# Two fused feed-forward blocks behind linear attention: where the tiles lie in SBUF

## The chip, the cores and the metric

The kernel runs on one core of a Trainium2 chip. The metric is the device time of one execution in microseconds, as the median of several runs; beside it stands one execution recorded by the hardware profiler, and all durations of single instructions come from that one.

## The reference

For 8 batches, 8 heads, 576 positions and 64 features per head:

```
kv  = einsum(k, v)                 # per head, 64 x 64
out = q @ kv                       # linear attention, no softmax
x   = out / rms(out) * g_norm      # then 4608 tokens x 512
h   = x @ w_in                     # 512 -> 2048
g   = P(h) / (Q(h) + 1e-6)         # cubic over 1 + |b0||h| + |b1|h^2
y   = g @ w_out                    # 2048 -> 512
z   = silu(y @ w_gate) * (y @ w_val)   # 512 -> 1536, two products
o   = z @ w_o2                     # 1536 -> 512
```

All data is float32.

## The kernel before

Every large product is made exact to float32 by splitting both factors into a high and a low part and multiplying three times (`mm3`, L103 to L107: high by high, high by low, low by high). All tiles are 128 partitions deep; the 4608 tokens are 9 tiles of 512. A matmul names two things in SBUF: the weights that are loaded into the array and the operand that is streamed past them (the moving operand).

**Stage 1** (to about 916 us) is a loop over 144 steps, 9 tiles of tokens by 16 chunks of `w_in`/`w_out`. A step runs 12 matmuls of `h_mm` (tile `ph`; weights `wt` in pool `w`, moving operand `x` in pool `x`) and 12 of `y_mm` for the chunk two steps earlier (tile `y`; weights `wt`, moving operand `ghl` in pool `g`). Between them, in small pieces, stands the attention of the next tile (tiles `qhl`, `kvh`, `kvl`, `sqhl` in pool `attn`). ScalarE, VectorE and GpSimd work out the rational function and write `ghl`. `y` goes to DRAM.

**Stage 2** (916 to about 1457 us) makes the gate and value products in 12 chunks of `w_gate`/`w_val`. A chunk's weights are a unit `u0` to `u5` (tile `wu`, 14 KiB per partition: seven 256-wide blocks as high and low part; chunks 6 to 11 use the units again). Token tiles, split, lie in a rotation of nine slots of 8 KiB (`slots`, L498: four in pool `x`, five in pool `ring`), and `x_slot` hands them out in turn. Three token tiles go "direct" (`direct_mm`, L584: for each of 6 chunks f and 3 tiles n, 24 matmuls, with x slots 0 to 5 as moving operand); the others go in pairs through a Strassen-like scheme of seven products of 6 matmuls (`product`, L601; 48 steps, 6 of them with 256 columns in place of 512). The first direct products stand between the last two `y_mm` of stage 1 (L880 to L884).

**Stage 3** (from 1457 us) multiplies by `w_o2`: the roles change, weights are the token slots, and the moving operand `wo` lies in the units `u0` to `u5`, three chunks in each (`o_mm`, L721).

What the vector engines do between the products is a hand-written order: `put(q, f, n, op)` hangs an operation behind step n of chunk f. In the direct part, chunk f+1's raw weights (pool `late`, tags `crg` and `crv`, two buffers each) are fetched by `u_fetch` (L437, on SyncE's queue), prepared by `u_scale` and `u_join`, split into the unit by `u_direct` (L464: two ScalarE copies and two GpSimd subtractions of 512 columns), and summed by `u_early` (four VectorE operations of 256 columns) into `sm` tiles, which `u_late` later splits into the rest of the unit. `u_direct(0)` runs in the last tile of stage 1.

Pools are stacks from two sides: a pool with `side="left"` lies above the ones opened before it, one with `side="right"` below them. By the pools' sizes a partition is laid out so (KiB from its start):

| | stage 1 | stages 2 and 3 |
|---|---|---|
| left, rising | const 1 to 2.8, w 2.8 to 130.8, g to 138.8, e to 150.8, stg to 158.8 | const, out 2.8 to 10.8, work to 24.8, ring to 64.8, raw to 88.8, units u1 to u5 to 158.8 |
| right, falling | x 192 to 224, attn 164 to 192 | x 192 to 224, late 162 to 192 (crg, crv, and u0 at 178 to 192) |

In pool `attn`, `kvh` and `kvl` lie at 164 to 172 and `qhl` and `sqhl` at 178 to 182.

Of the kernel before, what the change touches and what calls it, by code (L numbers as in the profile page):

```python
# [8 lines left out]
F32 = mybir.dt.float32  # L9
F32R = mybir.dt.float32r  # L10
# [30 lines left out]
def fused_kernel(ctx: ExitStack, tc: tile.TileContext, kv_main, kv_left, q_t, w_in, w_out, w_gate, w_val, w_o2, ab, g_norm, out):  # L41
# [14 lines left out]
    PS = bass.MemoryType.PSUM  # L56

    const = ctx.enter_context(tc.tile_pool(name="const", bufs=1, side="left"))
    a_ctx = ExitStack()
    w_p = a_ctx.enter_context(tc.tile_pool(name="w", bufs=1, side="left"))  # L60
    g_p = a_ctx.enter_context(tc.tile_pool(name="g", bufs=2, side="left"))
    e_p = a_ctx.enter_context(tc.tile_pool(name="e", bufs=2, side="left"))
    s_p = a_ctx.enter_context(tc.tile_pool(name="stg", bufs=2, side="left"))
    x_p = ctx.enter_context(tc.tile_pool(name="x", bufs=1, side="right"))
    d_p = ctx.enter_context(tc.tile_pool(name="dram", bufs=1, space=bass.MemoryType.DRAM))
    ps_y = ctx.enter_context(tc.tile_pool(name="ps_y", bufs=1, space=PS))
    ps_h = ctx.enter_context(tc.tile_pool(name="ps_h", bufs=2, space=PS))
# [35 lines left out]
    def mm3(ps, wh, wl, xh, xl, first, last, more=False):  # L103

        nc.tensor.matmul(ps, lhsT=wh, rhs=xh, start=first, stop=False, skip_group_check=more)  # L105
        nc.tensor.matmul(ps, lhsT=wh, rhs=xl, start=False, stop=False, skip_group_check=more)  # L106
        nc.tensor.matmul(ps, lhsT=wl, rhs=xh, start=False, stop=last, skip_group_check=more)  # L107
# [254 lines left out]
            c = slice(m * P, m * P + P)  # L362
            mm3(yps[m], w[:, 0, c], w[:, 1, c], g[:, 0, :], g[:, 1, :], f == 0, f == NF1 - 1)

    def evac_pair(dst, j, pool, tag, alone=False):
        sb = pool.tile([P, 2, N], F32, tag=tag, name="sb")
        act(sb[:, 0, :], yps[2 * j])
        if alone:
            nc.sync.dma_start(out=dst[:, 0, :], in_=sb[:, 0, :])
        nc.vector.tensor_copy(out=sb[:, 1, :], in_=yps[2 * j + 1])  # L370
        if alone:
            nc.sync.dma_start(out=dst[:, 1, :], in_=sb[:, 1, :])
        else:
            nc.sync.dma_start(out=dst, in_=sb)

    def y_evac(t, pool, tag):
        for j in range(2):
            evac_pair(y_dram[t][j], j, pool, tag)

    mid = {}  # L380

# [44 lines left out]
    def halves_of(ap):  # L426
        return ap.rearrange("p (a n) -> p a n", a=2)
# [2 lines left out]
    HK = DM // 2  # L430
    raw_u = {}
    val = {}
    sums = {}
    wu = {}
    w_dram = {f: d_p.tile([P, 2, N], F32, name=f"wd{f}") for f in range(UP, NF2)}
# [12 lines left out]
    def u_join(f, compact=False):  # L448

        if not compact:  # L450
            run(join_ops(raw_u[f]), 2)
            val[f] = [w_views(r)[2] for r in raw_u.pop(f)]
            return
        c = late["out"].tile([P, 2, N], F32, tag="g", name="wc")
        for j, r in enumerate(raw_u.pop(f)):
            lo, hi, _ = w_views(r)
            stt(c[:, j, :].bitcast(I32), hi, 3, lo, ALU.logical_shift_left, ALU.bitwise_or)
        nc.sync.dma_start(out=w_dram[f], in_=c)

    def u_halves(u, src, at, eng):  # L460
        act(u[:, 0, at, :], src)
        sub(eng, u[:, 1, at, :], src, u[:, 0, at, :])

    def u_direct(f, eng):  # L464

        g, v = val[f]
        u = wu[f] = late[f"u{f % UP}"].tile([P, 2, 7, HK], F32R, tag=f"u{f % UP}", name="wu")
        u_halves(u, halves_of(g), slice(0, 7, 6), eng)
        u_halves(u, halves_of(v), slice(4, 6), eng)

    def u_sums(f, tiles):
# [110 lines left out]
        return bank["d"][m % 2 * 2:m % 2 * 2 + 2]  # L582

    def direct_mm(f, n, ps, parts=2, part=0):  # L584
        u = wu[f]
        for b, at in ((0, (0, 6)), (1, (4, 5)))[part:part + parts]:
            for j in range(2):
                for kk in range(2):
                    c, x = slice(kk * P, kk * P + P), xc["D", 2 * n + j]
                    first, last = j + kk == 0, j + kk == 2  # L590
                    mm3(ps[b], u[:, 0, at[j], c], u[:, 1, at[j], c], x[:, kk, 0, :], x[:, kk, 1, :], first, last)
        return ps

    def direct_post(f, n, ps):
# [14 lines left out]
    def wid(i):  # L609
        return width[seq[steps[i][0]]]  # L610
# [17 lines left out]
    def post(i, n):  # L628

        if i < 0:  # L630
            return
        if n == 0:
            merge(i, 2, "c", ALU.subtract, "d")
            merge(i, 3, "c")
        elif n == 2:
            sv[i, "g"] = late["out"].tile([P, 2, wid(i)], F32, tag="g", name="gout")
            act(sv[i, "g"][:, 0, :], sv[i, "d"], AF.Silu)
            act(sv[i, "g"][:, 1, :], sv[i, "c"], AF.Silu)
        elif n == 3:
            g = sv[i, "g"]  # L640
            mul(g[:, 0, :], g[:, 0, :], sv[i, "a"])
        elif n == 4:
            g, (q, f) = sv[i, "g"], steps[i]
            merge(i, 3, "b")
            mul(g[:, 1, :], g[:, 1, :], sv[i, "b"])
            for h, (t, o) in enumerate(halves[seq[q]]):
                nc.sync.dma_start(out=g_dram[t, f][:, o:o + wid(i)], in_=g[:, h, :])
# [87 lines left out]
    def o_evac(n):  # L735
        t = order[n]
        o = out[t * N:(t + 1) * N, :].rearrange("(j m p) n -> j p m n", j=2, p=P)
        for m in range(4):
            yps[m] = banks(len(steps) + n)[m]
        for j in range(2):  # L740
            evac_pair(o[j], j, late["out"], "g", n == TILES - 1)

    with tc.manual_schedule():
        nc.vector.memset(bias_r, EPS_RMS)
# [89 lines left out]
        for s in range(S1):  # L834
            t, f = divmod(s, NF1)
            if s == S1 - NF1:
                attn_ctx.close()
                late["p"] = late["u0"] = ctx.enter_context(tc.tile_pool(name="late", bufs=1, side="right", reuse_waits="tile"))
                u_fetch(0)
                u_fetch(1)  # L840
            done = kv_n[1]
            h_mm(s)
            if s >= LAG:
                y_mm(s - LAG)
            attn_pe(s)
            if t == TILES - 1 and f == 2:
                u_scale(0)
            if kv_b:
                kv_evac(*kv_b)
                kv_b = None  # L850
            if t == 0 and f in (0, 3, 4, 7, 8, 11):
                pkv = ps_a.tile([P, HP, P], F32, tag="pa1", name="pkv")
                kv_b = (kv_jobs[kv_n[1]][0], pkv)
                for _ in range(HP):
                    kv_mm(pkv)
            g_step(s, raws[:2] if t == 0 else raw_u[0][f - 3:f - 2] if t == TILES - 1 and 3 <= f < 5 else ())
            if s >= LAG and f == LAG - 1:
                y_evac((s - LAG) // NF1, s_p, "stg")
            attn_tail(s)
            if t == 0:  # L860
                k = len(raws[:2])
                wa_split(k)
                for w in raws[:2]:
                    w_scale(w)
                wa_fetch(2)
                kv_load(4, done)
            if t == TILES - 1:
                if f == 5:
                    val[0] = [w_views(r)[2] for r in raw_u.pop(0)]
                    u_direct(0, nc.gpsimd)  # L870
                elif f in (6, 7):
                    raw_x["D", f - 6] = y_fetch(0, f - 6, 0, N, s_p, "stg")
                    xc["D", f - 6] = x_slot(N)
                elif 8 <= f < 12:
                    k, c = divmod(f - 8, 2)
                    split(xc["D", k][:, c, :, :], raw_x["D", k][:, c, :], nc.gpsimd)
                elif f == 12:
                    u_scale(1)
# [7 lines left out]

        a_ctx.close()
        b_pools = {}
        for name in ("out", "work", "ring", "raw", "units"):
            b_pools[name] = ctx.enter_context(  # L890
                tc.tile_pool(name=name, bufs=2 if name == "out" else 1, side="left", reuse_waits="tile")
            )
        late.update(b_pools)
        for f in range(1, UP):
            late[f"u{f}"] = b_pools["units"]
        DVE, POOL = nc.vector, nc.gpsimd

        for n, tag in enumerate(("b11", "b12", "b21", "b22"), 2):
            raw_x["D", n] = y_fetch(n // 2, n % 2, 0, N, late["raw"], tag)
        for n in range(2, 4):  # L900
            x_split(("D", n), raw_x["D", n], DVE)
        direct_post(0, 0, direct_ps)
        for n in range(4, 6):
            x_split(("D", n), raw_x["D", n], DVE)
        u_early(0)
        y_evac(TILES - 1, late["out"], "g")


        for f in range(UP):
            nxt = f + 1 < UP  # L910
            if nxt:
                if f:
                    put(0, f, 0, partial(u_scale, f + 1), partial(u_late, f - 1, DVE))
                put(0, f, 0, partial(u_join, f + 1), partial(u_direct, f + 1, POOL))
                put(0, f, 1, partial(u_early, f + 1))
                put(0, f, 2, partial(u_scale, UP + f), partial(u_join, UP + f, True))
            put(0, f, 0, partial(u_fetch, UP + f))
            if nxt and f + 2 < UP:
                put(0, f, 1, partial(u_fetch, f + 2))
        put(0, UP - 1, 0, partial(u_late, UP - 2, DVE))  # L920
        put(1, 0, 3, partial(u_scale, NF2 - 1))
        put(1, 0, 5, partial(u_join, NF2 - 1, True))
# [174 lines left out]
```

## Time and profile before

| what | value |
|---|---|
| time, median of 3 runs | 1763.37 us (1760.73 to 1764.11) |
| time of the profiled execution | 1761.45 us |
| its span, first to last instruction | 1759.7 us |
| mean granted TensorE clock | 0.999 |
| busy share of TensorE / VectorE / ScalarE / GpSimd | 99% / 70% / 57% / 29% |

TensorE's matmuls overlap: one lasts about 390 ns in the record, and the next begins some 230 ns after it. So what a matmul costs in a stretch in which TensorE never pauses is read from the stretch's length and the number of matmuls in it, not from the mean duration. The number that the view gives for a stretch takes in the matmul that is still running when the stretch begins, so one is taken off.

### The profile page before, as it was taken

What the parts mean: (1) busy time and instruction counts of PE and PEld (TensorE: products, weight loads), DVE (VectorE), ACT (ScalarE), POOL (GpSimd) and SP (SyncE); (2) the same over time, 40 slices, a digit from 0 to 9 for tenths busy, and PEclk for the clock granted to TensorE, in tenths of its full rate; (3) what the DMA queues carried; (4) which work ended last, traced back from release to release, by engine and by line L of the source; (5) the groups of instructions that cost most, each with busy time, mean ns of one, the idle gap of its engine ahead of it and who ended that gap; (6) DMA issues with size and microseconds to landing.
All of it is one profiled execution on the core that took longest, in us unless ns stands there. A gap on an engine that the chain in (4) does not pass through costs nothing.

```text
span 1759.7 us, 21291 instructions
## 1 busy us (share of the span) xinstructions
PE 1739.4 (99%) x7792; PEld 1419.9 (81%) x7792; DVE 1235.6 (70%) x1625; ACT 998.2 (57%) x1662; POOL 505.0 (29%) x361
## 2 busy tenths in 40 slices
PE   8998999999999999999999999999999999999999
PEld 6776888888888888888888888888888888888887
DVE  5989999998989898998886656756546756212211
ACT  5777777787877787777773434444424445112110
POOL 3556444444434343443331212223102212000000
PEclk9999999999999999999999999999999999999999
DMA  9763100010101000011117436122542255423411
GB/s 307 246 211 110 36 12 32 13 37 13 37 12 37 12 31 12 13 48 37 60 37 259 178 132 269 66 96 72 182 165 102 102 186 194 177 96 123 165 48 48
DMA packets 68681, 176.50 MB, mean 100 GB/s; under 512 B 7649, under 2 KB 10209, under 8 KB 66785
## 3 DMA queue, kind: packets, MB, share of 16 engines
q1 hardware_dynamic: 68576, 175.15, 28.4%
q8 instruction: 61, 1.00, 0.2%
q14 instruction: 44, 0.35, 0.1%
HBM read 117.44 MB, written 57.67 MB: 100 GB/s over the span
## 4 chain that ended last, share of the span: by engine, by line
PE 51%; issue 1%; DVE 0%; DMA 0%; POOL 0%; ACT 0%; SPq 0%; DVEq 0%; POOLq 0%; ACTq 0%
PE pb L105 10%; PE pb L107 10%; PE pb L106 10%; PE pb L731 6%; PE pb L733 6%; PE pb L732 6%; PE y L106 1%; PE y L107 1%; PE y L105 1%; PE ph L106 1%; PE ph L107 1%; PE ph L105 1%; DVE e L424 0%; DMA yraw<-yd 0%; POOL xc L94 0%
## 5 line engine op out<-in xcount | busy, mean ns | idle before, releaser
L94 POOL TENSOR_TENSOR ghl<-e,ghl 128x512 fp32r<-128x512 f32 x144 | 190.9, 1326 | 473.7 <-issue 261.6
L105 PE MATMUL pb<-xc,wu 128*128 128x512 f32 (+1 forms) x816 | 310.9, 381 | 1.0 <-DVE e L424 1.0
L107 PE MATMUL pb<-xc,wu 128*128 128x512 f32 (+1 forms) x816 | 310.8, 381 | 0.0
L106 PE MATMUL pb<-xc,wu 128*128 128x512 f32 (+1 forms) x816 | 310.6, 381 | 0.0
L101 DVE SCALAR_TENSOR_TENSOR e<-e,e 128x512 f32<-128x512 f32 x288 | 257.3, 893 | 34.5 <-ACT e L91 29.6
L106 PE MATMUL y<-ghl,wt 128*128 128x512 f32 x576 | 226.5, 393 | 4.0 <-POOL ghl L94 3.9
L105 PE MATMUL ph<-x,wt 128*128 128x512 f32 x576 | 229.6, 399 | 0.0
L106 PE MATMUL ph<-x,wt 128*128 128x512 f32 x576 | 227.3, 395 | 1.1 <-POOL x L94 1.1
L107 PE MATMUL ph<-x,wt 128*128 128x512 f32 x576 | 227.5, 395 | 0.0
L105 PE MATMUL y<-ghl,wt 128*128 128x512 f32 x576 | 225.7, 392 | 1.6 <-ACT ghl L91 1.6
L107 PE MATMUL y<-ghl,wt 128*128 128x512 f32 x576 | 226.4, 393 | 0.0
L424 DVE TENSOR_TENSOR e<-e,pb 128x512 f32<-128x512 f32 (+1 forms) x192 | 124.5, 653 | 144.1 <-PE pb L107 87.9
L91 ACT ACTIVATE e<-pb 128x512 f32<-128x512 f32 (+1 forms) x144 | 82.2, 571 | 238.7 <-PE pb L107 225.6
L105 PEld LDWEIGHTS pb<-xc,wu 128*128 128x128 f32 x816 | 153.3, 188 | 32.5 <-DVE e L424 1.6
L106 PEld LDWEIGHTS pb<-xc,wu 128*128 128x128 f32 x816 | 153.3, 188 | 31.1
L107 PEld LDWEIGHTS pb<-xc,wu 128*128 128x128 f32 x816 | 153.2, 188 | 30.9
L732 PE MATMUL pb<-wo,xc 128*128 128x512 f32 x432 | 169.3, 392 | 0.0
L731 PE MATMUL pb<-wo,xc 128*128 128x512 f32 x432 | 169.3, 392 | 0.0
L733 PE MATMUL pb<-wo,xc 128*128 128x512 f32 x432 | 169.2, 392 | 0.0
L91 ACT ACTIVATE e<-ph 128x512 f32<-128x512 f32 x144 | 85.6, 595 | 137.5 <-PE ph L107 136.9
L370 DVE COPY sb<-pb 128x512 f32<-128x512 f32 x18 | 12.5, 692 | 201.7 <-PE pb L733 201.7
L101 DVE SCALAR_TENSOR_TENSOR e<-e,na,e 128x512 f32<-128x512 f32 x144 | 148.0, 1028 | 0.0
(120 smaller groups left out, 3130.8 us busy)
## 6 DMA issues: line engine op xcount, KB each, us to landing
graw<-gd SPq DMA_DIRECT2D x108, 256.0 KB, 4.6
gd<-gout SPq DMA_DIRECT2D x84, 256.0 KB, 2.0
kvm<-in_kv_main SPq DMA_DIRECT2D x32, 512.0 KB, 9.1
yraw<-yd SPq DMA_DIRECT2D x26, 512.0 KB, 5.5
q<-in_q_t SPq DMA_DIRECT2D x36, 256.0 KB, 2.6
yd<-sb SPq DMA_DIRECT2D x18, 512.0 KB, 3.4
wraw<-in_w_in SPq DMA_DIRECT2D x16, 512.0 KB, 6.5
wraw<-in_w_out SPq DMA_DIRECT2D x16, 512.0 KB, 4.0
```

The source lines that it names most:

```text
L91: nc.scalar.activation(out=out, in_=in_, func=func, **kw)
L94: eng.tensor_tensor(out=out, in0=a, in1=b.bitcast(F32), op=ALU.subtract)
L101: nc.vector.scalar_tensor_tensor(out=out, in0=in0, scalar=scalar, in1=in1, op0=op0, op1=op1)
L105: nc.tensor.matmul(ps, lhsT=wh, rhs=xh, start=first, stop=False, skip_group_check=more)
L106: nc.tensor.matmul(ps, lhsT=wh, rhs=xl, start=False, stop=False, skip_group_check=more)
L107: nc.tensor.matmul(ps, lhsT=wl, rhs=xh, start=False, stop=last, skip_group_check=more)
L370: nc.vector.tensor_copy(out=sb[:, 1, :], in_=yps[2 * j + 1])
L424: eng.tensor_tensor(out=out, in0=a, in1=b, op=op)
L731: nc.tensor.matmul(b[m], lhsT=gh, rhs=w[:, 0, :], start=f == 0, stop=False)
L732: nc.tensor.matmul(b[m], lhsT=gh, rhs=w[:, 1, :], start=False, stop=False)
L733: nc.tensor.matmul(b[m], lhsT=gl, rhs=w[:, 0, :], start=False, stop=f == NF2 - 1)
```

## The change

The pools are laid out anew, and little else is done. In stage 1 pool `x` moves from the top to right above `const`, and `w`, `g`, `e` and `stg` move up by its 32 KiB. In stages 2 and 3 the left side is, from below, `x`, `ring`, `units` with all six units, `raw`, `work`; pool `out` is gone, and its tag `g` (results on their way out) lies in `late`, at the top. By the pools' sizes:

| | stage 1 | stages 2 and 3 |
|---|---|---|
| left, rising | const 1 to 2.8, x 2.8 to 34.8, w to 162.8, g to 170.8, e to 182.8, stg to 190.8 | const, x 2.8 to 34.8, ring to 74.8, units u0 to u5 to 158.8, raw to 182.8, work to 196.8 |
| right, falling | attn 196 to 224 | late 200 to 224 (crg, crv, g) |

Because `u0` now lies where stage 1's `w` still is, chunk 0's direct weights are split into two tiles of tag `g` first (`u_first`), its direct products read those, and `u_again` writes the three of the blocks that later products need into `u0` once stage 1 is over; `u_early(0)` moves behind `u_early(1)`. The raw token tiles for the second and third direct tile go into two ring slots in place of `raw`, and the last `y` leaves through two tags of `raw`.

```diff
     const = ctx.enter_context(tc.tile_pool(name="const", bufs=1, side="left"))
+    x_p = ctx.enter_context(tc.tile_pool(name="x", bufs=1, side="left"))
     a_ctx = ExitStack()
...
-    x_p = ctx.enter_context(tc.tile_pool(name="x", bufs=1, side="right"))
...
-    def evac_pair(dst, j, pool, tag, alone=False):
-        sb = pool.tile([P, 2, N], F32, tag=tag, name="sb")
+    def evac_pair(dst, j, pool, tag, bufs, alone=False):
+        sb = pool.tile([P, 2, N], F32, tag=tag, bufs=bufs, name="sb")
...
-        c = late["out"].tile([P, 2, N], F32, tag="g", name="wc")
+        c = late["p"].tile([P, 2, N], F32, tag="g", bufs=2, name="wc")
...
+    def u_first(eng):
+
+        for src in val[0]:
+            t = late["p"].tile([P, 2, 2, HK], F32R, tag="g", bufs=2, name="wu0")
+            act(t[:, 0], halves_of(src))
+            sub(eng, t[:, 1], halves_of(src), t[:, 0])
+            first_u.append(t)
+
+    def u_again(eng):
+
+        g, v = val[0]
+        u = wu[0] = late["u0"].tile([P, 2, 7, HK], F32R, tag="u0", name="wu")
+        u_halves(u, halves_of(g)[:, 1:2, :], slice(6, 7), eng)
+        u_halves(u, halves_of(v), slice(4, 6), eng)
...
     def direct_mm(f, n, ps, parts=2, part=0):
-        u = wu[f]
-        for b, at in ((0, (0, 6)), (1, (4, 5)))[part:part + parts]:
+        def w(b, hl, j, c):
+            return wu[f][:, hl, ((0, 6), (4, 5))[b][j], c] if f else first_u[b][:, hl, j, c]
+
+        for b in range(part, part + parts):
...
-                    mm3(ps[b], u[:, 0, at[j], c], u[:, 1, at[j], c], x[:, kk, 0, :], x[:, kk, 1, :], first, last)
+                    mm3(ps[b], w(b, 0, j, c), w(b, 1, j, c), x[:, kk, 0, :], x[:, kk, 1, :], first, last)
...
-            sv[i, "g"] = late["out"].tile([P, 2, wid(i)], F32, tag="g", name="gout")
+            sv[i, "g"] = late["p"].tile([P, 2, wid(i)], F32, tag="g", bufs=2, name="gout")
...
-            evac_pair(o[j], j, late["out"], "g", n == TILES - 1)
+            evac_pair(o[j], j, late["p"], "g", 2, n == TILES - 1)
...
-                late["p"] = late["u0"] = ctx.enter_context(tc.tile_pool(name="late", bufs=1, side="right", reuse_waits="tile"))
+                late["p"] = ctx.enter_context(tc.tile_pool(name="late", bufs=1, side="right", reuse_waits="tile"))
...
-                    u_direct(0, nc.gpsimd)
+                    u_first(nc.gpsimd)
...
-        for name in ("out", "work", "ring", "raw", "units"):
+        for name in ("ring", "units", "raw", "work"):
             b_pools[name] = ctx.enter_context(
-                tc.tile_pool(name=name, bufs=2 if name == "out" else 1, side="left", reuse_waits="tile")
+                tc.tile_pool(name=name, bufs=1, side="left", reuse_waits="tile")
             )
         late.update(b_pools)
-        for f in range(1, UP):
+        for f in range(UP):
             late[f"u{f}"] = b_pools["units"]
...
-        for n, tag in enumerate(("b11", "b12", "b21", "b22"), 2):
-            raw_x["D", n] = y_fetch(n // 2, n % 2, 0, N, late["raw"], tag)
+        for t in (1, 2):
+            pool, tag = slots[6 + t]
+            r = late["ring"].tile([P, 2, 2, N], F32, tag=tag, name="yraw")
+            for j in range(2):
+                raw_x["D", 2 * t + j] = r[:, j]
+                nc.sync.dma_start(out=r[:, j], in_=y_dram[t][j])
...
-        u_early(0)
-        y_evac(TILES - 1, late["out"], "g")
+        for j in range(2):
+            evac_pair(y_dram[TILES - 1][j], j, late["raw"], ("t2", "t3")[j], 1)
...
+        put(0, 0, 0, partial(u_again, POOL))
+        put(0, 0, 1, partial(u_early, 0))
```

## Rows read from the trace of the kernel before

**Rows 1.** The page: its first line, and busy time by engine (us, share, instructions).

```profile
span 1759.7 us, 21291 instructions
...
PE 1739.4 (99%) x7792; PEld 1419.9 (81%) x7792; DVE 1235.6 (70%) x1625; ACT 998.2 (57%) x1662; POOL 505.0 (29%) x361
```

**Rows 2.** Busy time by stretch, TensorE: stretch, us, PE (instructions), clock, DMA share, GB/s.

```profile
937.95:949.14 11.20, 11.20 (x49) 1.00 0.91 331
1262.17:1283.53 21.36, 21.36 (x182) 1.00 0.87 315
1474.75:1491.49 16.74, 16.74 (x73) 1.00 0.41 128
1499.75:1524.28 24.53, 24.53 (x109) 1.00 0.23 85
1524.28:1532.45 8.16, 8.16 (x37) 1.00 0.89 303
1546.44:1557.36 10.92, 10.92 (x49) 1.00 0.00 0
```

**Rows 3.** The same columns, stages 2 and 3 in three long stretches.

```profile
932.35:1246.90 314.55, 314.55 (x1368) 1.00 0.42 152
1283.53:1456.81 173.28, 173.28 (x758) 1.00 0.38 135
1456.81:1755.49 298.68, 298.68 (x1302) 1.00 0.34 118
```

**Rows 4.** The same columns, stage 1: a y, an h and a y.

```profile
490.26:493.03 2.77, 2.77 (x13) 1.00 0.00 0
493.03:495.82 2.79, 2.79 (x13) 1.00 0.00 0
495.82:498.56 2.74, 2.74 (x13) 1.00 0.37 96
```

**Rows 5.** Groups by line in stretches from 733.85, 1524.29 and 493.04 us: busy us, mean ns.

```profile
L105 PE MATMUL po<-qhl,kvh 128*128 128x512 f32 x1 | 0.4, 393 | 0.0
L106 PE MATMUL po<-qhl,kvh 128*128 128x512 f32 x1 | 0.4, 389 | 0.0
...
L731 PE MATMUL pb<-wo,xc 128*128 128x512 f32 x1 | 0.4, 393 | 0.0
L732 PE MATMUL pb<-wo,xc 128*128 128x512 f32 x1 | 0.4, 389 | 0.0
...
L105 PE MATMUL ph<-x,wt 128*128 128x512 f32 x1 | 0.4, 395 | 0.0
...
L106 PE MATMUL ph<-x,wt 128*128 128x512 f32 x1 | 0.4, 387 | 0.0
```

**Rows 6.** Instructions in order of time, the DMA queue: start us, us.

```profile
930.55 0.63 SPq L441 DMA_DIRECT2D wraw<-in_w_gate  x1
```

**Rows 7.** The same columns: VectorE, ScalarE, GpSimd, TensorE around the first chunks.

```profile
928.46 0.42 DVE L424 TENSOR_TENSOR sm<-wraw,sm 128x256 f32<-128x256 f32 x1
...
935.03 0.42 DVE L424 TENSOR_TENSOR sm<-wraw,sm 128x256 f32<-128x256 f32 x1
...
936.62 0.68 ACT L91 ACTIVATE wraw<-wraw 128x512 f32<-128x512 f32 x1 [0.68 <-DMA wraw<-in_w_gate]
...
947.75 2.60 POOL L94 TENSOR_TENSOR wu<-wraw,wu 128x512 fp32r<-128x512 f32 x2 [13.71 <-ACT wu L91]
...
954.60 0.40 PE L105 MATMUL pb<-xc,wu 128*128 128x512 f32 x1
```

**Rows 8.** Groups by line, whole span: ScalarE, GpSimd, VectorE.

```profile
L91 ACT ACTIVATE wu<-wraw 128x512 fp32r<-128x512 f32 x12 | 7.6, 673 | 16.3 <-DVE wraw L101 16.3
...
L94 POOL TENSOR_TENSOR wu<-wraw,wu 128x512 fp32r<-128x512 f32 x12 | 16.0, 1356 | 53.4 <-ACT wu L91 53.4
...
L101 DVE SCALAR_TENSOR_TENSOR e<-e,na,ph 128x512 f32<-128x512 f32 x144 | 107.4, 746 | 4.0
...
L101 DVE SCALAR_TENSOR_TENSOR u<-po,g_neg,r 128x512 f32<-128x512 f32 x32 | 23.8, 745 | 0.0
```

## What the change should do: the forecast

> **What bounds the kernel now.** First the page: TensorE is busy for 99% of the span, the next engine, VectorE, for 70% [rows 1]. So a change is worth what it takes from or adds to TensorE's own pace, unless it makes TensorE wait. The pace is therefore what I read next, in stretches in which TensorE never pauses, cut so that in each one all weights lie in one part of SBUF and all moving operands in one part. I call a place low up to 158.8 KiB and high from 164 KiB, and a matmul mixed when its weights and its moving operand lie in different parts. The reader is to see four kinds side by side [rows 2]: moving high, weights low (937.95, units u1 and u2, slots in `x`): 11.20 us for 48 matmuls, 233.3 ns each. Moving low, weights high (1474.75, stage 3): 16.74 / 72 = 232.5. Both low (1499.75 and 1546.44): 24.53 / 108 = 227.1 and 10.92 / 48 = 227.5, each with a few slower ones at its start. Both high (1524.28): 8.16 / 36 = 226.7. The granted clock is 1.00 in all of them, so it is not the clock. Nor is it DMA traffic: the DMA share is 0.91 in a mixed stretch and 0.89 in the one where both are high, 0.41 in a mixed one and 0.00 to 0.23 in those where both are low. What goes with the 6 ns is the place. Two of the stretches that differ, 1474.75 and 1499.75, run the same three lines of code over the same kind of tiles.
>
> Stage 1 has the same sign: 12 `h` matmuls (x high, weights low) take 2.79 us, 12 `y` matmuls (both low) 2.74 or 2.77 [rows 4].
>
> **The change part by part.** *Stages 2 and 3.* Following the nine slots and six units through the program, 1554 of the 3492 matmuls of 512 columns are mixed: 264 in the direct part (240 with slots 0 to 3 against u1 to u5, 24 with slots 4 and 5 against u0), 750 in the seven-product steps, 540 in stage 3. (The shares alone, 4 slots of 9 and 1 unit of 6, give 46%; the count is 45%.) After the change slots and units all lie under 158.8 KiB, where both-low matmuls already run in the trace. The room is best read whole: three long stretches [rows 3] hold 1367, 757 and 1301 matmuls (one taken off each). At 226.7 ns they would take 309.90, 171.61 and 294.94 us and take 314.55, 173.28 and 298.68. That is 4.65 + 1.67 + 3.74 = 10.1 us. It agrees with 1554 x 6.6 ns = 10.3.
>
> Not all of it goes. Chunk 0's direct weights now come from tag `g` at the top, and their moving operands are low, so its 72 matmuls are all mixed; 48 of them were both high. That costs 48 x 6.6 ns = 0.3 us, and 24 that stay mixed keep 0.2 us of the room. Net gain 9.6 us. The 256-column steps take 21.36 / 181 = 118 ns mixed [rows 2]; no row shows them unmixed. Half of a 512-column matmul would be 113, so 210 mixed ones can give 0 to 1.0 us; I take 0, because 118 is already above half of the mixed rate, which says that something other than the columns paces them.
>
> *Stage 1.* `x` comes down beside `w`: `h` is unmixed. But `g` goes up, to 162.8 to 170.8 KiB, and `w` ends at 162.8. Whether `y` becomes mixed hangs on where high begins, between 158.8 (u5, low) and 178 (u0, high). The only reads in the gap are `kvh` and `kvl` at 164 to 172 as weights against `qhl` at 178. If they were low, the stretch would be mixed. Entering a both-high stretch from a both-low one, the first two matmuls last 393 and 389 ns; entering a mixed one, 395 and 387 the second and third pair of [rows 5]. The attention product gives 393 and 389 the first pair of [rows 5]. So I count 164 upward as high, and `g` with it: `y` becomes mixed as `h` ceases to be. The two exchange roles. 144 steps of 2.79 for `h` and half 2.74, half 2.77 for `y` become 2.79 for `y` and 2.74 to 2.77 for `h`: between 2.2 us less and 2.2 us more. In the trace the 2.77 stands where attention matmuls cut in ahead of the h/y pair, so that the pair starts out of step. Now the mixed run always follows the unmixed one at once, and I take a value nearer to the good end: 1.3 us less.
>
> *Operations added and moved.* `u_first` has the same two copies and two subtractions as `u_direct(0)` had, at 0.67 and 1.36 us [rows 8]; nothing changes. `u_again` adds a 512- and a 256-column copy on ScalarE (1.35 us at most) and as many subtractions on GpSimd (2.7 us at most), behind `u_direct(1)`. GpSimd was idle for 13.71 us before its next work there [rows 7], which hides it; without that cover it would push `u_direct(2)` back by its own length. The four raw token loads are the same four DMAs into other tiles, and the last `y` goes out in the same two DMAs.
>
> One wait is new. `crg` and `crv` have two buffers, held by chunks 0 and 1. `u_fetch(6)`, which needs one, was issued at 930.55 [rows 6], after `u_early(0)` had ended at 928.46 + 0.42 [rows 7]. Now `u_early(0)` stands behind `u_early(1)`, which ends at 935.45, and takes 4 x 0.42: the fetch can be issued between 935.5 and 937.1, up to 6.6 us later. Behind it on SyncE's queue stand the direct results' stores, `u_fetch(2)` and the four loads of the next pair. ScalarE was already waiting for that very fetch at 936.62 [rows 7], so its lateness goes through ScalarE to `u_scale(2)`, VectorE's join, and `u_direct(2)`, which ended at 947.75 + 2.60 = 950.35; TensorE wanted the unit at 954.60 [rows 7]. The slack is 4.25 us, so the price is 0 to 2.4 us. It comes once, since a stall moves the later needs by as much. ScalarE's and VectorE's idle time in this part swallows some of the 6.6; I take 0.4.
>
> VectorE and ScalarE work on other addresses too, `e` now high. The same operation took 746 ns on low tiles and 745 on high ones [rows 8]: no price.
>
> **The sum.** -9.6 - 1.3 + 0.4 = -10.5 us. Against the profiled execution's own 1761.45 us (span 1759.7) that is 1751.0; the median of the runs, 1763.37, stands 1.9 us above that execution, so the forecast median is 1752.9.
>
> **The rivals.** *`g` still counts as low* (the border lies above 171 KiB). Then nothing in stage 1 is mixed, and a step's 24 matmuls at 226.7 ns take 5.44 us in place of 2.79 + 2.755: 0.105 x 144 = 15 us, somewhat less where TensorE waits for its first data, say 14. Time 1763.4 - 9.6 + 0.4 - 14 = 1740. For it: the gap holds few reads. Against it: the first pair of [rows 5].
>
> *The place costs nothing*, and what differs is some other thing that goes with those stretches. Nothing is gained, and 1763.4 + 0.4 = 1763.8. The Trainium skill speaks for this one: its page TensorE: Matmul & The Clock Gate, under Step-by-step: what each phase is for, says that TensorE has two independent SBUF read ports and that loading the next weights takes no read bandwidth from the running matmul, and the page SBUF — State Buffer, under Who interferes with whom, that TensorE never waits on anyone. Neither gives an address any price, and by them the time would be this rival's. Against it: four kinds of stretch that sort by place alone [rows 2].
>
> *The lowest 24 KiB are a third place.* No moving operand has been read there so far: ring began at 24.8. If x slots at 2.8 to 34.8 counted as mixed with everything above, `h` would stay at 2.79 and `y` rise to 2.79, 0.035 x 144 = 5 us more, and in stages 2 and 3 four slots of nine would be mixed with every unit, 44% as before: no gain. 1763.4 + 5 + 0.3 + 0.4 = 1769, slower. It decides from the point where stages 2 and 3 give back less than 2.2 us of their 10. Against it: weights at 2.8 to 24.8 ran with `ghl` at 131 to 139 without the 6 ns (the `y` rows of [rows 4] are of this layout).
>
> *The late fetch costs its full price or more*, because the stores behind it hold back tiles that VectorE needs: 2.4 to 5 us, 1755 to 1757.5.
>
> **How the numbers follow.** Forecast 0.72, `g` low 0.10, late fetch 0.07, place costs nothing 0.05, third place 0.04, something else 0.02. The forecast's own spread is that of stage 1 (plus or minus 2.2 around 0), the 256-column steps (1.0), the fetch (2) and the spread of the runs: 1748 to 1757. The range of 1745 to 1758 takes in the late fetch and leaves out `g` low, the third place and no price. A measurement of this kernel can tell about 0.2%, 3.5 us, from no change. Faster by more than that: 0.87, within it 0.07, slower 0.06.
>
> **What the changed profile would show.** Right: stretches of stage 3 all at about 227 ns per matmul, a whole stage 3 near 295 us, direct chunks 1 to 5 at 227, and chunk 0 at 233. In stage 1, 12 `y` at 2.79 us and 12 `h` at 2.74 to 2.77. SyncE's `u_fetch(6)` behind `u_early(0)`, and no gap on TensorE ahead of chunk 2's direct products. Wrong: `y` at 2.72 to 2.77 with `h` (the border is higher up), `h` still at 2.79 (place is not the cause, or the bottom is a place of its own), or pauses of TensorE between 930 and 960 us.

## The result, and the profile after

The median of 5 runs is 1746.45 us (1746.23 to 1749.53) against 1763.37 (1760.73 to 1764.38): ratio 0.9911, 95% interval 0.9897 to 0.9926, faster by 0.9%. The forecast of 1752.9 lay 6.45 us too high; the range of 1745 to 1758 holds the time. The profiled execution took 1747.46 us with a span of 1745.7, 14.0 less than before. The page's first line and its busy times:

```profile
span 1745.7 us, 21302 instructions
...
PE 1722.1 (99%) x7792; PEld 1421.7 (81%) x7792; DVE 1241.5 (71%) x1625; ACT 1001.1 (57%) x1664; POOL 505.9 (29%) x363
```

TensorE is still the bound, with the same 7792 matmuls in 17.3 us less busy time [rows 1]. Next the stretches, with the columns of [rows 2]: an `h`, a `y`, a direct product of chunk 0, the 256-column steps, the rest of stage 2 and stage 3.

```profile
488.12:490.84 2.72, 2.72 (x14) 1.00 0.00 0
490.84:493.56 2.72, 2.72 (x13) 1.00 0.38 96
904.79:907.58 2.79, 2.79 (x13) 1.00 0.00 0
1244.36:1275.87 31.51, 31.00 (x254) 1.00 0.70 256
1275.87:1446.63 170.76, 170.76 (x758) 1.00 0.39 137
1446.63:1741.52 294.89, 294.89 (x1302) 1.00 0.35 120
```

Three readings. Stage 3 takes 294.89 us where it took 298.68 [rows 3]: 294.89 / 1301 = 226.7 ns per matmul throughout. In stage 1 both `h` and `y` take 2.72 us, 226.7 ns per matmul, where they took 2.79 and 2.74 to 2.77 [rows 4]; the forecast had `y` going up to 2.79. (44 of the 144 `h`, each behind matmuls of the attention, still take 2.74 to 2.76.) Only chunk 0's direct products, with weights on the right side, still take 2.79 to 2.80. The 256-column stretch is as long as before (31.51 against 1283.53 - 1252.14 = 31.39).

Between stage 1 and stage 2, at the seam, something new appears. In order of time (start us, us, then the instruction, in brackets the idle time before it and what ended it):

```profile
915.66 0.39 PE L107 MATMUL y<-ghl,wt 128*128 128x512 f32 x1
916.08 1.74 SPq L921 DMA_DIRECT2D yraw<-yd  x4
919.27 1.06 ACT L91 ACTIVATE xc<-yraw 128x1024 fp32r<-128x1024 f32 x1 [10.54 <-DMA yraw<-yd]
920.36 1.23 DVE L94 TENSOR_TENSOR xc<-yraw,xc 128x1024 fp32r<-128x1024 f32 x1 [12.35 <-ACT xc L91]
...
920.38 0.79 PE L105 MATMUL pb<-xc,wu 128*128 128x512 f32 x1 [4.33 <-ACT xc L91]
...
921.64 0.79 PE L106 MATMUL pb<-xc,wu 128*128 128x512 f32 x1 [0.47 <-DVE xc L94]
...
922.23 0.63 PE L107 MATMUL pb<-xc,wu 128*128 128x512 f32 x1
```

The chain is read from the bottom up: TensorE waits 4.33 us for ScalarE's split of the second direct token tile, ScalarE has waited 10.54 us for its load from DRAM, and the load was issued at 916.08, when the last `y` matmul, begun at 915.66 and 0.39 us long, had just ended. Before, these four loads and the two of the first token tile were issued between 843 and 884 us. The stretches around the pause (fourth column: granted clock):

```profile
915.66:920.38 4.72, 0.39 (x2) 0.86 0.66 232
...
922.23:925.65 3.42, 3.42 (x10) 0.50 0.42 167
925.65:928.00 2.35, 2.35 (x11) 0.96 0.14 51
```

After the pause TensorE runs for some 5 us at the lower of its two clock levels, 1.2 GHz, with a matmul every 0.43 us.

So the 14.0 us come about in three parts. The first direct product begins at 904.79 instead of 915.99: 11.2 us won in stage 1. Chunk 1's first direct product begins at 934.58 instead of 937.95: of that lead, 7.8 us are lost again at the seam (4.5 in the pause, 3.1 in the eleven matmul intervals up to 925.98, the rest small). From there to the last matmul it is 806.9 us instead of 817.5: 10.6 won in stages 2 and 3.

### The profile page after: what moved, and what is told of

The parts are those of the page before. It is cut to its first block, busy times and chain, and to the rows that moved or that the text cites. A ratio compares the mean times of both kernels' runs of the same rounds, so it can differ in the third digit from the quotient of the medians.

```text
span 1745.7 us, 21302 instructions
## 1 busy us (share of the span) xinstructions
PE 1722.1 (99%) x7792; PEld 1421.7 (81%) x7792; DVE 1241.5 (71%) x1625; ACT 1001.1 (57%) x1664; POOL 505.9 (29%) x363
## 4 chain that ended last, share of the span: by engine, by line
PE 51%; issue 1%; DVE 0%; DMA 0%; POOL 0%; ACT 0%; SPq 0%; DVEq 0%; POOLq 0%; ACTq 0%
PE pb L106 10%; PE pb L105 10%; PE pb L107 10%; PE pb L749 6%; PE pb L751 6%; PE pb L750 6%; PE y L107 1%; PE y L105 1%; PE y L106 1%; PE ph L106 1%; PE ph L107 1%; PE ph L105 1%; DMA yraw<-yd 0%; DVE e L424 0%; POOL xc L94 0%
## 5 line engine op out<-in xcount | busy, mean ns | idle before, releaser
L101 DVE SCALAR_TENSOR_TENSOR e<-e,e 128x512 f32<-128x512 f32 x288 | 261.0, 906 | 30.7 <-ACT e L91 24.6
L105 PE MATMUL ph<-x,wt 128*128 128x512 f32 x576 | 227.1, 394 | 0.0
L106 PE MATMUL ph<-x,wt 128*128 128x512 f32 x576 | 225.0, 391 | 1.3 <-POOL x L94 1.3
L107 PE MATMUL ph<-x,wt 128*128 128x512 f32 x576 | 224.3, 389 | 0.0
```

Source lines behind the costliest of these rows:

```text
L101: nc.vector.scalar_tensor_tensor(out=out, in0=in0, scalar=scalar, in1=in1, op0=op0, op1=op1)
```

## The experiments

**The wait at the seam.** The slots' tags are laid out in order of first use, so the two that receive the raw token tiles lie lowest in `ring`, at 34.8 to 50.8 KiB. At the low end of this stretch stage 1 keeps the weights of its last `w_out` chunk, which the last `y` matmul reads. If that is the cause, other pools at this place remove the wait.

```diff
-        for name in ("ring", "units", "raw", "work"):
+        for name in ("units", "ring", "raw", "work"):
```

> The changed kernel with one word moved: units before ring in the list of pools, so that the two raw token tiles for the second and third direct tile land at 118.8 to 134.8 KiB in place of 34.8 to 50.8, where the changed kernel has the weight tile that the last y product reads. Theory (the loads wait for that last read): their four DMAs are issued before 880 us in place of 916 us, TensorE's two pauses behind the last y (4.3 and 0.5 us) and the half-clock matmuls after them are gone, and about 7.5 us with them: 1739. Rival (the pause comes from the late work of ScalarE or from chunk 0's weights, not from the loads): less than 1 us is gained.

Measured: 1737.83 us (1737.2 to 1740.93), ratio to before 0.9862 (0.9849 to 0.9876), 8.6 us less than with the change as it was made. The four loads now leave between 857 and 880 us, the first two of them 60 us ahead of the direct product that needs them first (917.06):

```profile
857.18 0.79 SPq L921 DMA_DIRECT2D yraw<-yd  x2
```

TensorE has no wait between 905 and 1000 us. In the profiles, the stretch from the first direct product to chunk 1's is 22.3 us long (905.95 to 928.22), where it is 29.8 with the change as it was made (904.79 to 934.58) and was 22.0 before. That the wait came from the place of the two tiles is shown, and so is its price: 7.5 us in the profiles, 8.6 between the medians. The 0.3 us that this stretch is still longer than before is what the forecast took for chunk 0.

**Is it the place in SBUF?** `y` had stayed fast although `g` lay at 162.8 to 170.8 KiB, above the place where I had put the border. Three experiments asked where the border lies. The first puts `g` still higher, to 182.8 to 190.8 KiB, by opening it last:

```diff
-    g_p = a_ctx.enter_context(tc.tile_pool(name="g", bufs=2, side="left"))
     e_p = a_ctx.enter_context(tc.tile_pool(name="e", bufs=2, side="left"))
     s_p = a_ctx.enter_context(tc.tile_pool(name="stg", bufs=2, side="left"))
+    g_p = a_ctx.enter_context(tc.tile_pool(name="g", bufs=2, side="left"))
```

> The changed kernel with pool g opened after e and stg, so that ghl lies at 182.8 to 190.8 in place of 162.8 to 170.8 KiB. Theory (g was low in the changed kernel, the border is above 171 and below 183): y becomes mixed, 12 of them 2.79 us in place of 2.72, and the h after them 2.74: 9 to 12 us slower than the changed kernel, 1756 to 1758. Rival (place of g has no say, y is never mixed): as the changed kernel, 1746.

Measured: 1747.47 us, ratio 0.9920 (0.9906 to 0.9933), as with the change. An `h` and a `y`:

```profile
511.63:514.35 2.72, 2.72 (x14) 1.00 0.00 0
514.35:517.07 2.72, 2.72 (x13) 1.00 0.39 96
```

`y` is fast at a place where, before, unit `u0` (178 to 192) had been slow against low operands. One border, the same for weights and moving operand, can't give both.

The second takes the kernel before and moves pool `x` alone:

```diff
     const = ctx.enter_context(tc.tile_pool(name="const", bufs=1, side="left"))
+    x_p = ctx.enter_context(tc.tile_pool(name="x", bufs=1, side="left"))
...
-    x_p = ctx.enter_context(tc.tile_pool(name="x", bufs=1, side="right"))
```

> The kernel before with pool x alone moved to the left side, above const; all else keeps its order, so units u4 and u5 move to 162.8 to 176.8 and 176.8 to 190.8, and late with u0 to 194 to 224. Theory (one border, above 171 KiB): stage 1 gains the 11 us of the changed kernel, mixed matmuls of stages 2 and 3 fall from 1554 to 1056 (u0 and u5 against low slots, u0 in stage 3), 3.3 us less: 1749. Rival (weights count as high from 160 KiB on): u4 is mixed too, 2.4 us more: 1751, and u4's products run at 233 ns. The forecast's own reading (g high from 164 KiB on) does not bear on it, since g lies at 162.8 to 170.8 here as in the changed kernel.

Measured: 1744.2 us (1742.9 to 1746.47), ratio 0.9896 (0.9883 to 0.9910), better than the expectation by 5 us. A product of chunk 0, chunks 4 and 5 of the direct part, and 36 matmuls of stage 3 that read `u0`:

```profile
907.22:910.01 2.79, 2.79 (x13) 1.00 0.00 0
978.44:994.76 16.32, 16.32 (x73) 1.00 0.48 175
994.76:1011.08 16.32, 16.32 (x73) 1.00 0.40 145
1477.90:1486.29 8.39, 8.39 (x38) 1.00 1.02 375
```

`u4` and `u5` lie at 162.8 to 190.8 KiB here, on the left side, and run at 16.32 / 72 = 226.7 ns against low operands. `u0`, on the right side, still takes 8.39 / 36 = 233, now at 210 to 224 KiB; in the kernel before it took as much at 178 to 192, the height at which `u5` is fast. Only the side separates them, not the height.

The third leaves the kernel aside and sweeps the places in one tile:

```python
def group(n, w, x):
    for i in range(36):
        nc.tensor.matmul(ps[n % 4], lhsT=at(w + 0.5 * (i % 4), P), rhs=at(x, N), start=i == 0, stop=i == 35)
```

> No part of the reference is computed: groups of 36 matmuls of 512 columns over one tile that fills SBUF, weights fixed in a place (20, 210 or 166 KiB) and the moving operand swept from 4 to 220, then the moving operand fixed (60, 210, 166) and the weights swept; last the attention product's own places, weights 164 to 170 against 178 and 180. One border above 171: groups run at 226.7 ns when both are on one side and at 233 ns otherwise, the step at the same address for both operands, and the weights at 164 to 170 against 178 are mixed. Two borders (weights below 164, moving above 171): the steps lie at different addresses. A place of its own between: 166 goes at 226.7 with both sides.

Measured: every group at full clock takes 8.16 us, 226.7 ns per matmul. Here weights at 20 and 210 KiB, each with the moving operand at 60 and 212:

```profile
72.52:80.68 8.16, 8.16 (x37) 1.00 0.00 0
349.96:358.12 8.16, 8.16 (x37) 1.00 0.01 2
423.40:431.56 8.16, 8.16 (x37) 1.00 0.00 0
700.84:709.00 8.16, 8.16 (x37) 1.00 0.00 0
```

(The very first group, which begins at the lower clock, takes longer.) The place has no price at all. With that my explanation, in all its variants, had fallen, though its size in stages 2 and 3 was right.

**The start addresses.** What else differs between the sides? In this tile all starts are whole multiples of 512 bytes apart. In the kernel the tiles of one side are, too; but by the allocation (the profile shows no addresses) all tiles of the left side that the large products read start at 96 bytes modulo 256, that is, 96 bytes past a multiple of 256, and all of the right side at 224. So a matmul with operands on both sides has them 128 bytes apart modulo 256. This fits each row seen so far, also `kvh` against `qhl`, both on the right. The theory says that a tile of 128 bytes per partition, which nobody uses, is worth as much as the whole change. In the kernel before:

```diff
+    pad_p = ctx.enter_context(tc.tile_pool(name="pad", bufs=1, side="right"))
+    pad = pad_p.tile([P, 32], F32, name="pad")
     x_p = ctx.enter_context(tc.tile_pool(name="x", bufs=1, side="right"))
...
+        nc.vector.memset(pad, 0.0)
```

> The kernel before, with one tile of 128 bytes per partition opened first on the right side, so that every tile of the right side (x, attention, late with unit u0) starts 128 bytes lower and nothing else changes. By the theory of steps (a matmul costs 6 ns more when its weights and its moving operand start 128 bytes apart modulo 256; tiles of one side are whole multiples of 512 bytes apart, the two sides 128 bytes off) no matmul of the large products is off any more: stage 1 gains 11 us, stages 2 and 3 gain 10 us, no new wait: 1741 to 1743 us, with 12 h matmuls at 2.72 us and stage 3 near 227 ns per matmul. By any theory of places or of sides of SBUF nothing changes: 1763.

Measured: 1741.71 us (1739.25 to 1743.36), ratio 0.9882 (0.9869 to 0.9895). A `y`, an `h`, a direct product of chunk 0, the rest of stage 2, stage 3:

```profile
486.81:489.53 2.72, 2.72 (x13) 1.00 0.00 0
489.53:492.25 2.72, 2.72 (x13) 1.00 0.00 0
906.26:908.98 2.72, 2.72 (x13) 1.00 0.00 0
1269.29:1440.06 170.77, 170.77 (x759) 1.00 0.39 137
1440.06:1734.95 294.89, 294.89 (x1303) 1.00 0.34 120
```

With every pool where it was before, the last two stretches are as long as after the change, to 0.01 us. The same tile then goes where it should do harm: on the left, behind `x`, in the version with `units` ahead of `ring`.

```diff
     x_p = ctx.enter_context(tc.tile_pool(name="x", bufs=1, side="left"))
+    pad_p = ctx.enter_context(tc.tile_pool(name="pad", bufs=1, side="left"))
+    pad = pad_p.tile([P, 32], F32, name="pad")
```

> The version with units opened ahead of ring (1737.8), with the same tile of 128 bytes opened on the left side right after pool x, so that x stays and all other tiles of the left side start 128 bytes higher. All of them stay low and on the same side. By the theory of steps h is slow in stage 1 (144 x 12 matmuls at 232.9 in place of 226.7: +11 us), and in stages 2 and 3 the slots in x, 4 of 9, are off against every unit (some 1540 matmuls, +10 us): 1757 to 1760. By a theory of places, or of sides, nothing changes: 1737 to 1739.

Measured: 1762.03 us (1759.03 to 1767.06), ratio 0.9995 (0.9982 to 1.0008), a little over the upper end of what was expected: the whole gain is gone, with the layout of the change in place. An `h`, a `y`, and chunk 1 of the direct part:

```profile
483.34:486.13 2.79, 2.79 (x14) 1.00 0.00 0
486.13:488.87 2.74, 2.74 (x13) 1.00 0.00 0
...
939.42:956.07 16.65, 16.65 (x73) 1.00 0.97 351
```

`h` and `y` take what they took before [rows 4]; `y`, which follows each slow `h`, is itself at 2.74 and not 2.72, which I had not counted and which is about the size of the excess (0.02 x 144 = 3 us). On the right side, in the version with `units` ahead of `ring`, the tile should only help chunk 0:

> The version with units opened ahead of ring (1737.8), with the same tile of 128 bytes on the right side. By the theory of steps chunk 0's direct products, whose weights lie on the right side and whose moving operands on the left, come into step: 72 matmuls by 6 ns, 0.4 us less, 1737.4, with chunk 0's matmuls at 226.7 where TensorE does not wait. By a theory of places nothing changes: 1737.8. The two are told apart by the rows of chunk 0, not by the time.

Measured: 1741.11 us (1737.82 to 1743.66), ratio 0.9879 (0.9865 to 0.9892), 3.7 us over the expected time, but the interval overlaps that of the version without the tile, and the 0.4 us in question are too few for the time to show. The rows show them: chunk 0's product takes 2.72 us, where the version without the tile has 2.80 (905.95 to 908.75), and the stretch to chunk 1 is 21.8 us long (907.44 to 929.20) instead of 22.3:

```profile
907.44:910.16 2.72, 2.72 (x14) 1.00 0.00 0
```

**How far apart, and modulo what?** The probe again, with one operand stepped by 16 bytes:

```diff
-        for w in (20, 210, 166):
-            for x in FINE:
-                group(n, w, x)
+        for d in range(0, 1024, 16):
+            group(n, 20 * K + d, 60 * K)
+            n += 1
+        for d in range(0, 1024, 16):
+            group(n, 20 * K, 60 * K + d)
...
```

> Leaves out the whole computation: 208 groups of 36 matmuls of 512 columns over one tile that fills SBUF, the last group's sum is what is written out. In the first 64 groups the weights start at 20 KiB plus 0 to 1008 bytes in steps of 16, the moving operand at 60 KiB; in the next 64 the moving operand takes these steps; in the next 32 both do; in the last 48 the weights step by 32 bytes with weights or moving operand or both above 200 KiB. By the theory of steps groups with both starts equal modulo 256 take 226.7 ns per matmul, 36 of them 8.16 us, those 128 bytes apart 232.5 to 233.3, 8.4 us, the third set stays at 226.7 throughout, and the place makes no difference; between 0 and 128 it may rise in steps, and some difference may be better than 0. By a theory of places all groups of the first three sets take the same.

Weights moved by 16, 32, 128, 176, 192, 240 and 256 bytes; then the moving operand by 16, 128 and 256; then both by 16:

```profile
26.03:34.20 8.17, 8.17 (x38) 1.00 0.00 0
34.20:42.59 8.39, 8.39 (x38) 1.00 0.01 2
84.55:92.95 8.40, 8.40 (x37) 1.00 0.00 0
109.75:118.02 8.27, 8.27 (x37) 1.00 0.00 0
118.02:126.27 8.25, 8.25 (x38) 1.00 0.01 2
143.06:151.24 8.18, 8.18 (x38) 1.00 0.00 0
151.24:159.40 8.16, 8.16 (x38) 1.00 0.01 2
559.52:567.86 8.34, 8.34 (x38) 1.00 0.00 0
617.95:626.32 8.37, 8.37 (x38) 1.00 0.00 0
684.93:693.12 8.19, 8.19 (x37) 1.00 0.01 2
...
1093.95:1102.23 8.28, 8.28 (x38) 1.00 0.00 0
```

The price comes back with a period of 256 bytes. For the weights it is near nothing at 0, 16 and 240 bytes, about 0.1 us per 36 matmuls at 176 and 192, and some 0.2 to 0.3 (5 to 8 ns each) at all other steps. No offset was faster than 0, so there is no better step to look for. But the difference alone does not set the price. Weights 16 bytes further on cost nothing, while the moving operand 16 bytes further on costs 5 ns per matmul (8.34 us). And both 16 bytes further on, with no difference between them, cost 3 ns (8.28 us), where the expectation had nothing. Two controls in the kernel, with 256 bytes (`[P, 64]`) in place of 128: on the left, where 128 had cost 24 us (1762.0 against 1737.8),

> The version with units ahead of ring and a tile on the left side behind pool x, but of 256 bytes in place of 128. By the theory of steps x is in step with everything again, since only the difference modulo 256 counts: 1738 to 1741 us, 24 matmuls of stage 1 at 5.44 us, against 1762 with 128 bytes. If the tile itself or the shift of ring and units had cost the 22 us, it stays at 1760 or above.

gave 1742.8 us (1739.28 to 1746.91), ratio 0.9889 (0.9859 to 0.9920), 2 us over the expected end but far from 1762, with `h` and `y` at 2.72; and on the right in the kernel before,

> The kernel before with the tile on the right side, of 256 bytes in place of 128. By the theory of steps the two sides stay 128 bytes apart modulo 256 and nothing changes: 1763 us, h at 2.79 us. If it were the exact distance that counts, or the new tile itself that helped, it would be 1742 as with 128 bytes.

gave 1761.38 us (1759.21 to 1767.33), ratio 0.9988 (0.9973 to 1.0003): no gain that can be told. An `h` and a `y` of it:

```profile
503.81:506.60 2.79, 2.79 (x14) 1.00 0.03 9
...
506.60:509.34 2.74, 2.74 (x13) 1.00 0.00 0
```

So it is neither the tile nor the exact distance: what counts is where the two starts lie modulo 256. For the two remainders of this kernel, 96 and 224, equal is free and unequal costs 6 ns.

## Why the prediction was right, and where it was not

**Stages 2 and 3, -9.6: measured -10.6, or -10.3 with the 0.3 us that chunk 0 loses and that stand in the stretch before it.** The count of 1554 mixed matmuls and the price of 6.6 ns were right, since low and high happened to be left and right in the kernel before. The room was a little larger than 10.1 because the middle stretch of [rows 3] holds six matmuls of 256 columns, which I priced as whole ones. Chunk 0 stayed mixed, as forecast. The 256-column steps gave nothing, as taken, but the change hardly tests them: `x_split` puts the first four of the seven combinations of such a step into `late`, so 144 of their 252 matmuls are still mixed, where 210 were. The kernel before with the 128-byte tile has none mixed, and there 222 of them in a row take 26.64 us (1242.65 to 1269.29) against 26.34 before (1257.19 to 1283.53): at 256 columns equal starts gain nothing. (A slip without weight: the stretch at 937.95 reads unit u1 alone, not u1 and u2.)

**The cause failed:** "What goes with the 6 ns is the place." The stretches sorted by place, but as well by the side from which a tile was allocated, and so by its start address modulo 256. I had not looked for a second quantity that sorts them equally well. The probe of places found 226.7 ns everywhere, and 128 bytes of padding took the whole price away in the old layout.

**Stage 1, -1.3: measured -11.2.** The step that failed is "So I count 164 upward as high, and `g` with it: `y` becomes mixed". `kvh` and `qhl` were indeed not mixed, and I read the pair rightly; but they were so because both are on the right, and `g` stayed on the left. So `y` kept its equal starts while `h` got them. The rival with `g` low had the right outcome for `y`, but not the reason: with `g` put above 182 KiB `y` was just as fast. Its time of 1740 is one that the version without the wait at the seam, 1737.8, comes close to, though its stage 1 had 14 us and 11.2 were measured.

**The moved loads, 0: measured +7.5 (the stretch at the seam is 7.8 us longer, 0.3 of it chunk 0).** "The four raw token loads are the same four DMAs into other tiles" looked at the number of transfers and not at whose place the other tiles take. They had to wait for the last `y`. This was in none of the rivals. The version with `units` first shows it and gets 8.6 us back.

**The late fetch, +0.4: measured 0 to 0.2.** It was issued at 935.74, inside the forecast 935.5 to 937.1, but the seam had moved: it left 1.2 us after chunk 1's first product had begun, where it had left 7.4 us ahead of it. TensorE did not stop at chunk 2; at chunk 3 a weight load came 0.3 us late:

```profile
967.75 0.19 PEld L107 LDWEIGHTS pb<-xc,wu 128*128 128x128 f32 x1 [0.32 <-POOL wu L94]
```

That chunk took 16.51 us (967.24 to 983.75) where the one ahead of it took 16.33. In the version with `units` first, with the same order of fetches, chunks 1 to 5 all take 16.32: there the late fetch costs nothing.

**The sum.** -11.2 + 7.8 - 10.6 = -14.0 in the profiled spans, against -10.5. Two errors of about 9.9 and 7.4 us, of opposite sign, and 1.0 in stages 2 and 3 left 3.5 of difference. That the time fell into the range is luck: the reason for the gain was wrong, a gain in stage 1 and a wait at the seam were both missed, and without the wait it would have been near 1738, below the range. The other 2.9 of the 6.45 come from the runs: before, the median stands 1.9 above the profiled execution, after, 1.0 below it.

**What stays open.** Why unequal starts cost 6 ns isn't settled; the runs give the price, not the mechanism. The Trainium skill, page TensorE: Matmul & The Clock Gate, section Step-by-step: what each phase is for, gives TensorE two independent read ports, so that a weight load takes nothing from the running matmul; the steps of 16 bytes show a price that depends on both addresses (8.17 us with the weights moved by 16 bytes, 8.34 with the moving operand), of which it says nothing, and here the measurement decides. Its section Back-to-back issue gap gives N / 2.4 + 2.5 ns for an isolated warm matmul, an estimate of 215.8 for 512 columns; no group of the probe came under 226.7.

## What to carry to other kernels

When stretches of one kind run at two paces, list everything in which they differ, the start addresses modulo 256 bytes too, and test the cheapest: here 128 bytes of padding gave 1741.7 us in the old layout (ratio 0.9869 to 0.9895), and the whole new layout, with its wait removed, 1737.8 (0.9849 to 0.9876). When a tile is moved, ask who last reads its new place and when that read ends: the load into it can't start sooner, and the pause of TensorE that comes of it can cost more than its length: here the clock came back 5 us later than the work.

## What the hardware showed that I had not expected

A stream of 512-column matmuls with a weight load each costs 226.7 ns per matmul when the weights' and the moving operand's start addresses are equal modulo 256 (seen at 0, 96 and 224), and 232 to 234 at most other differences in steps of 16 bytes, 128 among them. Equal is not enough at every remainder: where both are 16 bytes off together it is 230 (8.28 us for 36). At 256 columns there is no such price (120.0 ns with equal starts, 118.6 with most of them 128 bytes apart). With starts that are multiples of 512 bytes apart, where in SBUF the operands lie makes no difference between 4 and 220 KiB. After a pause of 4.3 us the granted clock was 0.50, the 1.2 GHz level, until about 925.65, 5.3 us after the first matmul, and that cost 2.6 us on top of the two waits (3.1 for the eleven intervals less the second wait of 0.47).
